# A fused attention and feed-forward kernel: GpSimd's join of the global probabilities moves to the next slot, and a tile's output split moves ahead of the maxima

## The chip, the cores and the metric

The kernel runs on one core of a Trainium2 chip. Its time is the device time of one execution in microseconds (us), lower is better. A core has a matrix engine (PE, with its weight loads shown apart as PEld), a vector engine (DVE), a scalar engine (ACT), GpSimd (POOL) and a sync engine (SP) that here issues nearly all transfers. Each engine works through its own instructions in order; between engines, semaphores make one wait for another.

## The reference

Attention over 8 batches and 8 heads of size 64, with 512 local tokens and 32 global tokens each, followed by a feed-forward layer on all 4352 rows. Global queries see every key; local queries see the 32 global keys and the local keys at most 32 positions away.

```python
s_g = scale * np.matmul(q_g, k_all.transpose(0, 1, 3, 2))
out_g = np.matmul(sm(s_g), v_all)                  # 32 global queries, 544 keys
s_ll = np.where(mask, scale * q_l @ k_l.T, -1e9)   # mask: |i - j| <= 32
s_l = np.concatenate([scale * q_l @ k_g.T, s_ll], axis=-1)
out_l = np.matmul(sm(s_l), np.concatenate([v_g, v_l], axis=2))
x = concat([out_g, out_l]).transpose(0, 2, 1, 3).reshape(4352, 512)
h = np.maximum(x @ w_in, 0.0)                      # 512 -> 2048
out = (h * h) @ w_out                              # 2048 -> 512
```

## The kernel before

**Tiles and slots.** A tile is 256 local queries of one head, so there are 16 groups (batch and half of the sequence) of 8 heads, 128 tiles in all. The main loop (line 605) runs one slot for each t from 0 to 145. Slot t begins tile t's attention, ends that of tile t-1, and runs step m = t-9 of the feed-forward layer: 17 blocks of 256 rows with 8 steps each (16 blocks of local rows, and a last one of the 256 global rows). Block k uses the outputs of group k. The last of its tiles, 8k+7, gets its output split (`x_evac`, line 278) in slot 8k+9, the very slot of the block's step 0; these are the slots with t % 8 == 1.

**Precision.** From tile 16 on, products are made of float32 split into two float32r parts. ACT writes the high part by a copy that rounds, DVE the rest by a subtraction. So each tile has pairs of such instructions: `qk` (queries and keys), `v` (values), `ph`/`pl`/`ml` (probabilities), `gh`/`gl` (hidden values), `x_h`/`x_l` (outputs).

**One slot, engine by engine** (from slot 17 on every engine keeps the order in which the program is written, `InOrder`, line 43):

- PE: the scores of tile t (`s<-qk`, line 155), the first product of the step (`h<-x_h`, `h<-x_l`, 24 matmuls in two halves, line 463), a score of the global queries (`gs`), the second product of the step before (`o<-ws`, 12 matmuls, line 497), then `av` of tile t-1 (`xa<-ph`, `xa<-ml`, `xa<-pl`, line 250). Some slots have one `g_av` (`gxo`, 13 matmuls) between the two halves of the second product.
- DVE: the two masked maxima of tile t (`softmax1`, writing `prob` from the scores), `x_l` of tile t-2, the rest of `v`, the normalisation (`softmax3`), then the jobs of place 3, then `parts_rest` of tile t-1 (`ph` on 32 partitions, `ml`, `pl`), `split_qk_rest` of tile t+1 (two subtractions named `qk`), in odd slots `g_evac` (`sg<-gs`), and `gl`.
- ACT: `x_h`, the high part of `v`, the two exponentials, the high part `ph`, jobs of place 3, the high part `qk` of tile t+1, the two activations of the hidden values (`pt<-h`, `pt<-pt`) and `gh`.
- POOL: `join` of tile t-1, one copy that puts the turned planes together again (`joined<-turned`), then `turn` of tile t, three copies that take the normalised probabilities apart into two 16-bit planes (`planes<-prob`).
- SP: the transposing DMA of tile t (`turned<-planes`, issued in `turn`), the load of tile t+2, and loads and stores of other jobs.

The transposition of a tile's probabilities is thus: `prob` normalised by DVE, three POOL copies, a DMA, one POOL copy in the next slot, ACT's `ph`, DVE's parts, and `av` on PE near the end of that slot.

**Global queries.** Four heads of a batch make one unit of 32 x 4 = 128 rows and 544 keys, 16 units in all, two for each batch. Its scores are gathered in `sg` over the slots before. Its other work is put into slots by a table by hand (line 680): each entry has a slot, a place in the slot, and a function. The slot d is t for the first unit of a batch and t+2 for the second, so that the units of batch after batch have their slot d+2 at t % 16 = 13 and 3. Places 4 and 3 come behind `load_head` (line 641), place 2 behind `g_evac`, places 0 and 1 inside and behind the second product. The entries that matter here:

```python
(d + 2, 3, g_norm),         # DVE: sum, reciprocal; then g_turn
(d + 3, 3, g_split_v, 0),   # ACT gvh, DVE gvl and gvh
(d + 3, 2, g_parts),        # ACT pth, DVE ptl and pth
(d + 3, 2, g_load_v, 1),
(d + 4, 0, g_av, 0),        # PE gxo
```

`g_turn` (line 374), called by `g_norm`, does for a unit what `turn` and `join` do for a tile, and does it in one go: a POOL copy of `sg` into planes (`gp<-sg`), a transposing DMA (`gq<-gp`) that SP issues behind the tile's own and behind a load, and a POOL copy back into `sg` (`sg<-gq`). POOL's next instruction is `join` of the same slot's tile, in slot d+3. I call slot d+2 the norm slot, d+3 the join slot and d+4 the parts slot.

Of the kernel before, what the change touches and what calls it, by code (L numbers as in the profile page):

```python
# [10 lines left out]
U16 = mybir.dt.uint16  # L11
# [9 lines left out]
NT = NGR * H  # L21
# [8 lines left out]
NPLAIN = 16  # L30
# [8 lines left out]
def f(ap):  # L39
    return ap.bitcast(F32)  # L40
# [19 lines left out]
def attention_moe(  # L60
# [22 lines left out]
    def plain(t):  # L83
        return t < NPLAIN
# [3 lines left out]
    def w_take(n):  # L88
        w_bufs["free"] -= n

    def load_head(t):
        if plain(t):
            w_take(1)
            raw = wp.tile([P, 1024], F32, tag="w", name=f"raw{t}")[:, :PK]
        else:
            raw = p2.tile([P, PS], F32, tag="raw", name=f"raw{t}")
        if t == 0:
            nc.sync.dma_start(raw[:, : QC + KC], pk[t, :, : QC + KC])
        else:
            sp.dma_start(raw, pk[t, :, : raw.shape[1]])  # L100
        heads[t] = dict(raw=raw)
# [16 lines left out]
    sg = cp.tile([P, 2, 640], F32, name="sg")  # L118
# [30 lines left out]
    def split_v(t):  # L149
        raw = heads[t]["raw"]  # L150
        v = heads[t]["v"] = p2.tile([P, 2, 192], F32R, tag="v", name=f"v{t}")
        ac.copy(v[:, 0, :], raw[:, QK:])
        ve.tensor_sub(v[:, 1, :], raw[:, QK:], f(v[:, 0, :]))

    def scores(t):
        hd = heads[t]
        pool, tag = (ps_h, "h") if t < 8 and t % 2 else (ps_a, "s")
        s = pool.tile([P, 2, WIN], F32, tag=tag, name=f"s{t}")
        for u in range(2):
            qs, ks = slice(KC + u * P, KC + u * P + P), slice(128 * u, 128 * u + WIN)  # L160
            if plain(t):
                pe.matmul(s[:, u, :], hd["raw"][:, qs], hd["raw"][:, ks], start=True, stop=True)
            else:
                pe.matmul(s[:, u, :], hd["hi"][:, qs], hd["hi"][:, ks], start=True, stop=False)
                pe.matmul(s[:, u, :], hd["lo"][:, u * P : u * P + P], hd["hi"][:, ks], start=False, stop=True)
        hd["s"] = s
# [46 lines left out]
    def transposes(t):  # L213
        pr = heads[t]["pr"]
        for i, (o, n) in enumerate(((0, 128), (320, 128), (128, 96), (224, 96))):
            pe.transpose(pt[:n, 128 * i : 128 * i + 128], pr[:, o : o + n], ident)

    def pt_copy(t):
        pts = p2.tile([P, 512], F32, tag="gh", name=f"pts{t}")
        ac.copy(pts, pt)  # L220
        heads[t]["pts"] = pts
# [9 lines left out]
    def join(t):  # L231
        words = joined.bitcast(U16).rearrange("p (n h) -> p h n", h=2)
        po.tensor_copy(words, turned.rearrange("p (h c) n -> p h (c n)", h=2))
# [4 lines left out]
    def parts(t):  # L238

        ph = heads[t]["ph"] = p1.tile([P, 512], F32R, tag="ph", name=f"ph{t}")  # L240
        ac.copy(ph, joined)
# [36 lines left out]
    def x_evac(t):  # L278
        g, h = divmod(t, 8)
        xa = heads[t]["xa"]  # L280
        r = slice((h % 2) * 64, (h % 2) * 64 + 64)
        if g == 0:
            ac.copy(xg[r, h // 2, :], xa)
        else:
            ac.copy(x_h[r, g % 2, h // 2, :], xa)
            ve.tensor_sub(x_l[r, g % 2, h // 2, :], xa, f(x_h[r, g % 2, h // 2, :]))
        heads[t] = None

    state = {}
# [84 lines left out]
    def g_turn(t, s):  # L374

        a = p1.tile([P, 1280], U16, tag="pth", name=f"gp{t}")
        z = p1.tile([P, 10, P], U16, tag="ptl", name=f"gq{t}")
        words = s.bitcast(U16).rearrange("p (n h) -> p h n", h=2)
        po.tensor_copy(a.rearrange("p (h n) -> p h n", h=2), words)
        sp.dma_start_transpose(out=z, in_=a)  # L380
        po.tensor_copy(words, z.rearrange("p (h c) n -> p h (c n)", h=2))

    def g_parts(t):
# [194 lines left out]
    def w_need(m):  # L578

        if m < 8:  # L580
            while w_next["bits"] < 8 * m + 8:
                n = w_next["bits"]
                w_pass()
                assert w_next["bits"] > n
        elif m < 16:
            while not set(range(4 * (m - 8), 4 * (m - 8) + 4)) <= whi.keys():
                n = w_next["split"]
                w_chunk()
                assert w_next["split"] > n, (m, w_next, w_bufs, sorted(w_used)[-1:])
# [15 lines left out]
    for t in range(NSTEP + LAG + 1):  # L605
        m = t - LAG
        ve.on, ac.on, pe.on, po.on, sp.on = [t >= x for x in FREE]
        prev, run = 1 <= t <= NT, 0 <= m < NSTEP
        live, early = t < NT, t < NPLAIN
        if t < NPLAIN - 8:  # L610
            load_head(t + 8)
        if run:
            w_need(m)
        old = prev and plain(t - 1)
        new = prev and not old
        if old:
            transposes(t - 1)
        if new:
            join(t - 1)
        if live and not early:  # L620
            scores(t)
        if old:
            pt_copy(t - 1)
        if live:
            softmax1(t)
        if NPLAIN <= t - 2 < NT:
            x_evac(t - 2)
        if run:
            gemm1(m, 0)
        if live and not early:  # L630
            split_v(t)
        if live:
            softmax2(t)
        if new:
            parts(t - 1)
        if live and not early:
            softmax3(t)
            turn(t)
        if NPLAIN <= t + 2 < NT:
            load_head(t + 2)  # L640
        for place in (4, 3):
            for job, *args in jobs.pop((t, place), ()):
                job(*args)
        if 0 < m <= NSTEP and m % 8 == 1 and m > 8:
            evac(m // 8 - 1)
        w_tick(t, 0)
        if live and early:
            g_scores(t)
        if run:
            gemm1(m, 1)  # L650
        if old:
            av(t - 1)
        if live and not early:
            g_scores(t)
        if early and t + 1 < NPLAIN:
            scores(t + 1)
        if t + 1 < NT and not early:
            split_qk(t + 1)
        if run:
            act1(m)  # L660
        if old:
            x_evac(t - 1)
            w_take(-1)
        if early:
            softmax3(t)
        w_tick(t, 1)
        if t + 1 == NPLAIN:
            split_qk(t + 1)
        if new:
            parts_rest(t - 1)  # L670
        if t + 1 < NT:
            split_qk_rest(t + 1)
        if live:
            if t % 2 == 1:
                g_evac(t)
            if t % 4 == 3 and t + 1 < NT:
                g_load(t + 1)
        if live and t % 4 == 3 and (t // 8) % 2 == 1:
            d = t if t % 8 == 3 else t + 2
            for at, *job in (  # L680
                (d, 2, g_load_v, 0),
                (d + 1, 3, g_soft),
                (d + 1, 1, g_exp),
                (d + 2, 3, g_norm),
                (d + 3, 3, g_split_v, 0),
                (d + 3, 2, g_parts),
                (d + 3, 2, g_load_v, 1),
                (d + 4, 0, g_av, 0),
                (max(d + 5, 17), 3, g_x, 0),
                (d + 5, 2, g_split_v, 1),  # L690
                (max(d + 6, 17), 0, g_av, 1),
                (max(d + 7, 18), 3, g_x, 1),
            ):
                place, job, *args = job
                jobs.setdefault((at, place), []).append((job, t, *args))
        for job, *args in jobs.pop((t, 2), ()):
            job(*args)
        if m == NSTEP:
            for i in range(2):
                gemm2(m - 1, 0, (i,))  # L700
                gemm2(m - 1, 1, (i,))
                evac(NBLK - 1, (i,))
        elif m > 0:
            gemm2(m - 1, 0)
        for job, *args in jobs.pop((t, 0), ()):
            job(*args)
        if 0 < m < NSTEP:
            gemm2(m - 1, 1)
        if new:
            av(t - 1)  # L710
        if run:
            act2(m)
        w_tick(t, 2)
        for job, *args in jobs.pop((t, 1), ()):
            job(*args)
        if 0 < m <= 8:
            w_done(m - 1)
        w_tick(t, 3)
        if 8 * NGR - 2 <= m < 8 * NGR:
            cols = (slice(0, 224), slice(224, HALF))[m % 2]  # L720
            ac.copy(x_h[:, 0, :, cols], xg[:, :, cols])
            ve.tensor_sub(x_l[:, 0, :, cols], xg[:, :, cols], f(x_h[:, 0, :, cols]))
# [75 lines left out]
```

## Time and profile before

| what | value |
|---|---|
| median of 3 runs | 1126.45 us (1126.15 to 1127.83) |
| the profiled execution | 1123.84 us |
| its span, first to last instruction | 1122.1 us |
| mean granted PE clock over the span | 0.963 |
| busy: PE, PEld | 1052.1, 927.1 us |
| busy: DVE, ACT, POOL | 829.5, 720.4, 373.6 us |

Times in the trace are counted from the start of the span. A line of the timeline has start, duration, engine, source line (nearly all have line 53, that of the recording helper, so one goes by the names of tiles), operation, what is written from what, shapes and a count; in brackets stands how long the engine stood idle just before, and what ended that wait. A line of the windows view has a stretch of time, its length, the busy time of each engine in it with the number of its instructions, the granted PE clock (1.00 is full), the DMA engines' share and their GB/s. A line of the waits view has who waited for whom, the total, the count and the longest.

### The profile page before, as it was taken

What the parts mean: (1) busy time and instruction counts of PE and PEld (TensorE: products, weight loads), DVE (VectorE), ACT (ScalarE), POOL (GpSimd) and SP (SyncE); (2) the same over time, 40 slices, a digit from 0 to 9 for tenths busy, and PEclk for the clock granted to TensorE, in tenths of its full rate; (3) what the DMA queues carried; (4) which work ended last, traced back from release to release, by engine and by line L of the source; (5) the groups of instructions that cost most, each with busy time, mean ns of one, the idle gap of its engine ahead of it and who ended that gap; (6) DMA issues with size and microseconds to landing.
All of it is one profiled execution on the core that took longest, in us unless ns stands there. A gap on an engine that the chain in (4) does not pass through costs nothing.

```text
span 1122.1 us, 20557 instructions
## 1 busy us (share of the span) xinstructions
PE 1052.1 (94%) x7040; PEld 927.1 (83%) x7040; DVE 829.5 (74%) x2477; ACT 720.4 (64%) x1743; POOL 373.6 (33%) x496
## 2 busy tenths in 40 slices
PE   8999879998998989999998989989899899989998
PEld 6776669887997979878887879978798779979987
DVE  5688877787877878877887878878688878873310
ACT  6888667666776756766676666757576666654332
POOL 1001234433344343444344343443343433441000
PEclk9999989999999989989899999989899999989999
DMA  9782434455344544534445344445345354432000
GB/s 373 272 286 56 105 96 105 101 122 118 94 112 97 129 98 112 128 98 108 108 107 112 98 117 111 119 98 124 89 110 120 98 121 107 116 81 52 14 19 19
DMA packets 193576, 127.69 MB, mean 114 GB/s; under 512 B 143552, under 2 KB 168640, under 8 KB 193472
## 3 DMA queue, kind: packets, MB, share of 16 engines
q1 hardware_dynamic: 193328, 126.32, 43.8%
q8 instruction: 55, 0.90, 0.3%
q14 instruction: 49, 0.40, 0.1%
q10 hardware_dynamic: 144, 0.07, 0.0%
HBM read 82.84 MB, written 8.91 MB: 82 GB/s over the span
## 4 chain that ended last, share of the span: by engine, by line
PE 62%; DVE 14%; DMA 8%; ACT 6%; issue 6%; POOL 2%; SPq 0%; DVEq 0%; POOLq 0%; ACTq 0%
PE h L53 24%; PE o L53 23%; DMA gq<-gp 6%; PE s L53 6%; PE xa L53 5%; DVE prob L53 3%; PE gxo L53 2%; POOL joined L53 2%; DVE qk L53 2%; DVE ml L53 2%; PE gs L53 1%; DVE x_l L53 1%; DMA raw<-in_pk_dram 1%; DVE pl L53 1%; DVE st L53 1%
## 5 line engine op out<-in xcount | busy, mean ns | idle before, releaser
L53 PE MATMUL h<-x_h,ws 128*128 128x256 f32 x2048 | 409.0, 292 | 0.0
L53 PEld LDWEIGHTS h<-x_h,ws 128*128 128x128 f32 x2048 | 344.8, 201 | 0.7
L53 PE MATMUL o<-ws,gh 128*128 128x512 f32 x1024 | 322.6, 396 | 1.5 <-ACT ot L53 1.5
L53 PE MATMUL h<-x_l,ws 128*128 128x256 f32 x1024 | 299.9, 293 | 3.2 <-DVE x_l L53 3.2
L53 POOL COPY joined<-turned 128x1024 uint16<-128x1024 uint16 x112 | 158.8, 1418 | 321.0 <-DMA turned<-planes 123.8
L53 POOL COPY planes<-prob 128x448 uint16<-128x448 uint16 x336 | 163.3, 523 | 189.6 <-DVE prob L53 189.6
L53 PEld LDWEIGHTS h<-x_l,ws 128*128 128x128 f32 x1024 | 206.1, 201 | 6.7 <-DVE x_l L53 6.0
L53 PEld LDWEIGHTS o<-ws,gh 128*128 128x128 f32 x1024 | 182.6, 188 | 34.0 <-ACT ot L53 2.0
L53 PE MATMUL o<-ws,gl 128*128 128x512 f32 x512 | 201.8, 394 | 0.0
L53 ACT ACTIVATE prob<-prob,st 128x224 f32<-128x224 f32 x224 | 106.3, 476 | 88.2 <-DVE st L53 88.0
L53 DVE TENSOR_TENSOR gl<-pt,gh 128x512 fp32r<-128x512 f32 x128 | 88.1, 688 | 83.1 <-ACT gh L53 80.9
L53 PE MATMUL xa<-ph,v 128*64 128x128 f32 (+1 forms) x672 | 77.4, 247 | 46.6 <-DVE ph L53 24.2
L53 ACT CAST ph<-joined 128x512 fp32r<-128x512 f32 x112 | 68.3, 610 | 81.7 <-POOL joined L53 81.4
L53 ACT ACTIVATE pt<-h 128x512 f32<-128x512 f32 x128 | 74.5, 582 | 70.0 <-PE h L53 69.1
L53 DVE TENSOR_TENSOR qk<-raw,qk 64x352 fp32r<-64x352 f32 x224 | 113.0, 504 | 7.8 <-ACT qk L53 0.8
L53 DVE CUSTOM_DVE_ANT_0 prob<-s,con 128x224 f32<-128x224 f32 x224 | 78.2, 386 | 54.8 <-PE s L53 54.4
L53 PEld LDWEIGHTS xa<-ph,v 128*64 128x64 f32 x672 | 57.9, 137 | 69.4 <-ACT ph L53 28.4
L53 PEld LDWEIGHTS o<-ws,gl 128*128 128x128 f32 x512 | 96.0, 188 | 22.9
L53 ACT CAST x_h<-xa 64x256 fp32r<-64x256 f32 x120 | 43.7, 364 | 99.8 <-PE xa L53 99.2
L53 PE MATMUL s<-qk 128*128 128x224 f32 x448 | 89.5, 314 | 6.2 <-DVE qk L53 3.7
L53 ACT CAST qk<-raw 128x608 fp32r<-128x608 f32 x112 | 78.2, 698 | 9.6 <-DMA raw<-in_pk_dram 9.5
L53 PEld LDWEIGHTS s<-qk 128*128 128x128 f32 x448 | 66.1, 202 | 16.3 <-DVE qk L53 15.3
(86 smaller groups left out, 1585.4 us busy)
## 6 DMA issues: line engine op xcount, KB each, us to landing
raw<-in_pk_dram SPq DMA_DIRECT2D x112, 400.0 KB, 3.5
wr<-in_w_dram SPq DMA_DIRECT2D x32, 512.0 KB, 7.8
gv<-in_vg_dram SPq DMA_DIRECT2D x32, 320.0 KB, 3.7
out_dram<-ot SPq DMA_DIRECT2D x32, 256.0 KB, 2.5
raw<-in_pk_dram SPq DMA_DIRECT2D x15, 432.0 KB, 8.3
qr<-in_qg_dram SPq DMA_DIRECT2D x31, 64.0 KB, 3.2
turned<-planes SPq DMA_TRANSPOSE x112, 3.0
out_dram<-ot SPq DMA_DIRECT2D x8, 64.0 KB, 1.7
```

Of the source, the lines that this page charges most:

```text
L53: r = method(*args, **kwargs)
```

## The change

The last copy of `g_turn` becomes a function of its own, `g_join`, with an entry in the table for place 3 of the join slot, behind `g_split_v`; there it stands behind `join` of the tile before and behind the three copies of `turn` of the slot's own tile. `g_parts` goes from place 2 of the join slot to place 3 of the parts slot. And `x_evac` of tile t-2 (ACT's `x_h`, DVE's `x_l`) is written ahead of `softmax1` of tile t; on ACT that changes no order, since `softmax1` has nothing there, and on DVE `x_l` now stands ahead of the two maxima.

```diff
@@ def g_turn(t, s):
         po.tensor_copy(a.rearrange("p (h n) -> p h n", h=2), words)
         sp.dma_start_transpose(out=z, in_=a)
+        state["gq"] = z
+
+    def g_join(t):
+        words = sg[:, (t // 4) % 2, :].bitcast(U16).rearrange("p (n h) -> p h n", h=2)
+        z = state["gq"]
         po.tensor_copy(words, z.rearrange("p (h c) n -> p h (c n)", h=2))
...
         if old:
             pt_copy(t - 1)
+        if NPLAIN <= t - 2 < NT:
+            x_evac(t - 2)
         if live:
             softmax1(t)
-        if NPLAIN <= t - 2 < NT:
-            x_evac(t - 2)
         if run:
             gemm1(m, 0)
...
                 (d + 2, 3, g_norm),
                 (d + 3, 3, g_split_v, 0),
-                (d + 3, 2, g_parts),
                 (d + 3, 2, g_load_v, 1),
+                (d + 3, 3, g_join),
+                (d + 4, 3, g_parts),
                 (d + 4, 0, g_av, 0),
```

## The prediction

> **What bounds the kernel now.** I read the page first, then the waits, then the windows view by slots, and last the timeline of one unit.
>
> ```profile
> PE 1052.1 (94%) x7040; PEld 927.1 (83%) x7040; DVE 829.5 (74%) x2477; ACT 720.4 (64%) x1743; POOL 373.6 (33%) x496
> ...
> PE 62%; DVE 14%; DMA 8%; ACT 6%; issue 6%; POOL 2%; SPq 0%; DVEq 0%; POOLq 0%; ACTq 0%
> PE h L53 24%; PE o L53 23%; DMA gq<-gp 6%; PE s L53 6%; PE xa L53 5%; DVE prob L53 3%; PE gxo L53 2%; POOL joined L53 2%; DVE qk L53 2%; DVE ml L53 2%; PE gs L53 1%; DVE x_l L53 1%; DMA raw<-in_pk_dram 1%; DVE pl L53 1%; DVE st L53 1%
> ```
>
> PE looks full, but the chain that ended last leaves it for the transposition of the global probabilities (`gq<-gp`). The windows show what that costs: one plain slot, then a join slot and the sum of 13, then a parts slot and the sum of 12, last the first steady unit (slots 20 and 21). I cut slots where the scores' first matmul starts.
>
> ```profile
> 431.33:438.28 6.95, 6.95 (x53) 6.34 (x52) 5.67 (x20) 4.53 (x11) 2.56 (x4) 1.00 0.43 104
> ...
> 524.31:535.74 11.43, 8.25 (x53) 6.70 (x51) 6.23 (x21) 5.60 (x13) 3.98 (x5) 0.94 0.51 103
> sum 148.88, PE 107.53 PEld 86.60 DVE 80.94 ACT 71.75 POOL 51.79; mean PE 8.27 PEld 6.66 DVE 6.23 ACT 5.52 POOL 3.98
> ...
> 535.74:546.10 10.36, 10.36 (x63) 9.55 (x64) 8.66 (x21) 5.34 (x14) 3.71 (x5) 0.74 0.42 101
> sum 118.95, PE 118.47 PEld 108.90 DVE 106.15 ACT 65.90 POOL 43.78; mean PE 9.87 PEld 9.08 DVE 8.85 ACT 5.49 POOL 3.65
> ...
> sum 26.73, PE 18.19 PEld 15.66 DVE 16.45 ACT 12.68 POOL 7.18; mean PE 9.10 PEld 7.83 DVE 8.22 ACT 6.34 POOL 3.59
> ```
>
> A plain slot is 6.95 us and PE is busy in all of it. A join slot is 148.88/13 = 11.45 us with 8.27 busy: 4.50 too long. A parts slot is 118.95/12 = 9.91; 0.80 of its excess is the 13 `gxo` matmuls (a row below prices them), so 2.16 is loss, and there PE is "busy" because its clock is 0.74. A unit loses 6.66 us in these two slots. The last row: slots 20 and 21 lose 26.73 - 13.90 - 0.80 = 12.0.
>
> The timeline of the unit at 522 shows how (POOL's, PE's, ACT's and DVE's rows; the join slot begins at 524.31):
>
> ```profile
> 522.04 1.64 POOL L53 COPY gp<-sg 128x1280 uint16<-128x1280 uint16 x1
> 528.87 1.64 POOL L53 COPY sg<-gq 128x1280 uint16<-128x1280 uint16 x1 [5.18 <-DMA gq<-gp]
> 530.41 1.32 POOL L53 COPY joined<-turned 128x1024 uint16<-128x1024 uint16 x1
> 531.65 1.19 POOL L53 COPY planes<-prob 128x448 uint16<-128x448 uint16 x3
> 536.07 1.88 POOL L53 COPY joined<-turned 128x1024 uint16<-128x1024 uint16 x1 [3.22 <-DMA turned<-planes]
> ...
> 532.44 0.45 PE L53 MATMUL xa<-ph,v 128*64 128x128 f32 x4 [1.46 <-ACT ph L53]
> 534.54 0.69 PE L53 MATMUL xa<-ph,v 128*64 128x256 f32 x2 [1.65 <-DVE ph L53]
> ...
> 531.77 0.62 ACT L53 CAST ph<-joined 128x512 fp32r<-128x512 f32 x1 [4.46 <-POOL joined L53]
> 532.29 0.72 ACT L53 CAST gvh<-gv 128x640 fp32r<-128x640 f32 x1
> ...
> 522.60 1.92 DVE L53 TENSOR_TENSOR qk<-raw,qk 64x352 fp32r<-64x352 f32 x2
> 525.84 0.38 DVE L53 CUSTOM_DVE_ANT_0 prob<-s,con 128x224 f32<-128x224 f32 x1
> 527.75 0.58 DVE L53 TENSOR_SCALAR prob<-prob,st 128x224 f32<-128x224 f32 x2
> 533.05 0.69 DVE L53 TENSOR_TENSOR gvl<-gv,gvh 128x512 fp32r<-128x512 f32 x1 [4.72 <-ACT gvh L53]
> 536.06 0.68 DVE L53 TENSOR_TENSOR ptl<-sg,pth 128x512 fp32r<-128x512 f32 x1
> 536.76 1.28 DVE L53 TENSOR_TENSOR pth<-sg,pth 64x128 fp32r<-64x128 f32 x1
> ```
>
> POOL stands 5.18 us before a copy nobody needs yet; the tile's `joined` is queued behind it, ACT's `ph` behind that, DVE's and PE's work behind `ph`. Then both DVE splits of the unit are done while PE waits, and the half clock follows in the parts slot.
>
> **The change, part by part.**
>
> *`g_join` one slot later.* Removed from in front of `joined`: the wait and 1.6 us of copy. By the tile's own transposition `joined` would be ready early: at 536.07 it began 3.2 us after its `planes` ended, and in the norm slot `planes` ended at 522.1 (`gp` follows it), so it can start near 525.3 in place of 530.41, and `ph` right behind the exponentials. Added behind `planes` of the join slot: the same copy. `gq` lands, by POOL's row, at 528.87; the three `planes` follow the normalisation, which ended at 528.33, so `g_join` begins near 529.5 and ends near 531.1. The next `joined` needs its DMA, 3.2 us after `planes`, near 532.7. So POOL itself hides `g_join`; no DMA moves on SP's queue, as `g_join` issues none; but the load of `gv` for pair 1 still waits for DVE's `gvh`, and is wanted two slots later.
>
> *What is late next: DVE.* A plain slot's DVE rows:
>
> ```profile
> 432.13 0.39 DVE L53 CUSTOM_DVE_ANT_0 prob<-s,con 128x224 f32<-128x224 f32 x1 [1.13 <-PE s L53]
> 434.05 0.58 DVE L53 TENSOR_SCALAR prob<-prob,st 128x224 f32<-128x224 f32 x2
> 434.55 0.84 DVE L53 STREAM_TRANSPOSE xg<-gxs 32x32 f32<-32x32 f32 x4
> 436.67 0.98 DVE L53 TENSOR_TENSOR qk<-raw,qk 64x352 fp32r<-64x352 f32 x2
> 439.09 0.39 DVE L53 CUSTOM_DVE_ANT_0 prob<-s,con 128x224 f32<-128x224 f32 x1 [0.84 <-PE s L53]
> ```
>
> `qk` is done at 437.65 and the next scores start at 438.28: 0.63 of slack with 0.84 of transposes in the slot, so some 1.4 us may be added ahead of `qk` for nothing. The join slot adds `gvl` 0.69 and `gvh` 0.28 with gaps (1.0), and DVE enters it late: its maxima started at 525.84, 1.53 after the scores, not 0.80.
>
> To this comes a price that the old order hid. Beside `gp` (522.04 to 523.68) the pair `qk` took 1.92, in the plain slot 0.98; beside `joined` the 64x128 `pth` took 1.28. A DVE subtraction of two SBUF tiles that meets a POOL copy waits for its end. `sg<-gq` stood in DVE's idle 4.72 us; `g_join` will stand beside `gvl`, `gvh`, `ph`. Bounds: nothing, if it falls in the wait for ACT's `gvh`, to 1.64; I take 1.3, since it starts about when `gvl` ends. The Trainium skill's "SBUF — State Buffer" (the shared port pair) says the same as a rule, that a DVE instruction with two SBUF inputs and a GpSimd one that reads SBUF exclude each other and the loser waits for the whole instruction. By that rule the 1.64 would be the sum's term, 0.3 a unit more.
>
> So DVE reaches the end of `qk` in the join slot 1.0 + 1.3 + 0.8 (late entry) = 3.1 later than plain, against 1.4 of slack: 1.7 us of loss in place of 4.50.
>
> *`g_parts` in the parts slot.* ACT's `pth` 0.72 lies in ACT's slack (5.5 busy). DVE gets `ptl` 0.68 and `pth` 0.3 to 1.28 ahead of `ph`, `qk`; `gxo` gives PE 0.80 more. 1.0 + 0.3 (copies of `planes` beside them) - 0.8 - 1.4 is under zero, but DVE comes in late from the join slot. `gxo` stands behind the 24 `h` and half of the 12 `o`:
>
> ```profile
> 590.89 2.88 PE h L53 x24
> 593.91 2.80 PE o L53 x12
> ```
>
> With 0.5 for the scores it begins 4.9 us after them and needs DVE's `pth` only for its last matmul, near 5.6. The normalisation ends 3.3 after the scores (434.63); ACT's `pth`, 0.72 behind `ph`, and the two DVE splits bring me to 5.0 to 5.3, an estimate. I take 0.5 of loss in place of 2.16, bounds 0 and 2.2; most of the 2.16 was the half clock. In the slot after, DVE has 0.84 of transposes against the same slack: 0.
>
> So a unit loses about 2.2 where it lost 6.66: **4.45 gained**, 13 times (57.9; the parts slot missing among the 12 is taken like the others). Slots 20 and 21 carry weight splits (`ws`) on DVE as well; I take 4.5 lost of 12.0: **7.5 gained**. The unit of slot 13 lies in the phase that waits for weights, and the last, after the last tile, has no `joined` behind it: 0.
>
> *`x_l` ahead of the maxima.*
>
> ```profile
> PEld h L53 <- DVE x_l L53: 6.0, 14, 0.9
> PE h L53 <- DVE x_l L53: 3.2, 13, 0.7
> ...
> sum 51.50, PE 50.35 PEld 44.86 DVE 40.95 ACT 35.33 POOL 21.94; mean PE 7.19 PEld 6.41 DVE 5.85 ACT 5.05 POOL 3.13
> sum 50.06, PE 48.05 PEld 43.12 DVE 40.33 ACT 31.55 POOL 18.82; mean PE 8.01 PEld 7.19 DVE 6.72 ACT 5.26 POOL 3.14
> sum 54.29, PE 54.29 PEld 49.97 DVE 49.23 ACT 38.92 POOL 21.99; mean PE 7.76 PEld 7.14 DVE 7.03 ACT 5.56 POOL 3.14
> ```
>
> The sums are of the windows of slots t % 16 = 9 (7 of them, 7.36 each), 1 (6, 8.34) and 7 (7, 7.76). The last has 13 `gxo` and no loss, so `gxo` costs 0.80. Slots 9 and 1 are those where a block begins and PE waits for `x_l`: 0.41 and 0.58 too long. `x_l` will come some 0.7 earlier. I count 0.40 x 7 + 0.28 x 6 = **4.5 gained**; slot 1 gets half, as it starts with DVE late. Against it: the maxima wait for ACT's `x_h` and for `x_l`, 0.42 later where DVE is behind, 0.2 elsewhere (they wait 1.13 for the scores anyway); in a plain slot the 1.4 of slack covers it; in the join slot it is in the late entry.
>
> Sum: 57.9 + 7.5 + 4.5 = 69.9 less than the profiled execution's 1123.84 (span 1122.1 and 1.7 around it): 1053.9. The median of the runs is 2.6 above that execution, so I expect about **1055** between the two.
>
> **The rivals.**
>
> *PE's clock keeps falling.* The 1.7 us of join-slot loss still leaves PE idle in pieces. Speaking for it: pieces of 1.46 and 1.65 were enough for a parts slot at 0.74. A second mechanism of the same size goes with it: when DVE is late, the next `joined` slips between the two `qk` and holds the second for 1.3. Then a unit loses 4.7, and 13 x 1.96 = 25, 3 in slots 20 and 21 and 4 from `x_l` are gained: 1093. Against it, a slot with 0.98 of PE idle that kept its clock:
>
> ```profile
> 575.11:583.30 8.19, 7.21 (x53) 6.41 (x52) 6.28 (x16) 5.51 (x13) 3.13 (x4) 1.00 0.44 124
> ```
>
> The Trainium skill's "TensorE: Matmul & The Clock Gate" (what's actually happening) has the clock fall after an idle window of some 3.4 us; by that rule this rival would not occur, yet here two pieces of under 1.7 us sufficed. Chance 0.2.
>
> *All the loss goes.* If DVE's work is hidden wholly, a unit loses 0.5: 13 x 6.16 + 9.5 + 6 = 96, giving about 1030. For it: slots with 0.84 of transposes and a later split of `gv` still take 6.95. Chance 0.16.
>
> *The change doesn't free `joined`.* If `gq` landed after the next `joined` is due, POOL would wait as now, one slot later; it needs a landing 7 us or more after SP's issue.
>
> ```profile
> DMA to landing us min/median/max: 3.1/4.6/6.1
> ```
>
> The longest is 6.1, so chance 0.03, and the time 1115 to 1124.
>
> *Slower.*
>
> ```profile
> L53 ACT CAST x_h<-xa 64x256 fp32r<-64x256 f32 x120 | 43.7, 364 | 99.8 <-PE xa L53 99.2
> ...
> L53 DVE TENSOR_TENSOR x_l<-xa,x_h 64x256 fp32r<-64x256 f32 x120 | 49.7, 414 | 4.8 <-ACT x_h L53 3.0
> ```
>
> The maxima now stand behind `x_h` (0.36) and `x_l` (0.42). If nothing hid the two, each of 112 slots would lose 0.78, 87 us, against 65 from the units and slots 20 and 21: 1146. It turns against the kernel from 0.6 a slot. The 1.13 and 0.84 for which the maxima wait for scores, while `x_h` is ready, speak against it. Chance 0.03.
>
> **How the numbers follow.** Forecast 1055, chance 0.58; 1030: 0.16; 1093: 0.2; no release 0.03; slower 0.03. The forecast's own range, by its bounds of 1.0 to 3.3 a unit, is 1038 to 1070. The range for 8 in 10 takes in most of both neighbours: 1033 to 1093. About 0.2% (2.3 us) is what a measurement can tell from no change. Faster 0.95, same 0.02, slower 0.03.
>
> **What would show it.** Right: POOL's `sg<-gq` without a long wait, standing behind `planes`; `joined` of the norm slot's tile starting about 1 us after the scores; join slots of about 8.6 us and parts slots of 8.2; `gvl` or `gvh` or `ph` stretched beside `sg<-gq`; the wait of `h` for `x_l` nearly gone; plain slots still 6.95. Wrong: join slots over 10 us, a granted clock below 0.9 in parts slots, or plain slots above 7.0, which would be `x_l` on the path.

## The result, and the profile after

The changed kernel takes 1080.92 us (median of 4 runs, 1076.66 to 1085.06) against 1126.55 for the kernel before on the same chip: a ratio of 0.9593 [0.9555, 0.9631]. The profiled execution is the 1076.66. Forecast were 1055 and a range of 1033 to 1093. So the sign and the range held, and the size did not: the span fell by 1122.1 - 1074.9 = 47.2 us where 69.9 were forecast.

From the page of the changed kernel, the busy times and the shares of the chain that ended last:

```profile
PE 1031.6 (96%) x7040; PEld 908.9 (85%) x7040; DVE 853.1 (79%) x2477; ACT 718.1 (67%) x1743; POOL 382.1 (36%) x496
...
PE 41%; DVE 30%; ACT 13%; issue 7%; DMA 5%; POOL 4%; POOLq 0%; SPq 0%; DVEq 0%; ACTq 0%
PE o L53 17%; PE h L53 16%; DVE qk L53 5%; ACT prob L53 5%; DVE prob L53 4%; DVE ml L53 4%; DMA turned<-planes 4%; PE xa L53 3%; PE s L53 3%; DVE gl L53 3%; POOL joined L53 2%; DVE st L53 2%; ACT ph L53 2%; DVE x_l L53 2%; POOL planes L53 2%
```

The wait for `gq<-gp` (6% of the chain before) is no longer among the chain's items, as intended. But PE holds 41% of the chain where it held 62%, and the rest is not one engine: it runs through the tile's probabilities, `prob`, `planes`, `turned`, `joined`, `ph`, `ml`. That loop had a far smaller part of the chain before.

The view of cores gives span and mean granted clock, first of the kernel before, then of the changed one:

```profile
core 0: 1122.1 us, clock 0.963
```

```profile
core 0: 1074.9 us, clock 0.990
```

If PE was busy all the time that its clock was low, it lost (1 - 0.963) x 1122.1 = 41.5 us before and (1 - 0.990) x 1074.9 = 10.7 after. PE's busy time for the same 7040 matmuls fell by 1052.1 - 1031.6 = 20.5. So between 20 and 31 of the 47 us came back as clock, and the rest as fewer waits.

The first unit's join slot, by POOL's and DVE's rows of the timeline (the slot runs from 581.82 to 590.34), and its row in the windows view:

```profile
582.54 1.36 POOL L53 COPY joined<-turned 128x1024 uint16<-128x1024 uint16 x1 [1.81 <-DMA turned<-planes]
585.83 1.71 POOL L53 COPY planes<-prob 128x448 uint16<-128x448 uint16 x3 [1.93 <-DVE prob L53]
587.49 1.81 POOL L53 COPY sg<-gq 128x1280 uint16<-128x1280 uint16 x1
...
587.31 0.51 DVE L53 TENSOR_TENSOR ph<-joined,ph 32x256 fp32r<-32x256 f32 x1
587.85 1.55 DVE L53 TENSOR_TENSOR ml<-joined,ph 64x128 fp32r<-64x128 f32 x1
```

```profile
581.82:590.34 8.52, 7.85 (x50) 6.52 (x51) 7.63 (x21) 5.05 (x13) 4.83 (x5) 1.00 0.67 125
...
sum 59.65, PE 54.53 PEld 45.64 DVE 53.67 ACT 36.32 POOL 34.07; mean PE 7.79 PEld 6.52 DVE 7.67 ACT 5.19 POOL 4.87
...
sum 48.89, PE 48.36 PEld 43.56 DVE 42.38 ACT 35.08 POOL 18.43; mean PE 8.06 PEld 7.26 DVE 7.06 ACT 5.85 POOL 3.07
```

`joined` starts 0.72 us after the scores, `sg<-gq` stands behind `planes` with no wait at all, and one of DVE's subtractions beside it, `ml`, takes 1.55 in place of 0.28. It is so in six of the first units' seven join slots; in the seventh it is the first `qk` that meets the copy (1.78 in place of 0.52). The two sums are the first units' seven join slots, 59.65/7 = 8.52, and six parts slots, 48.89/6 = 8.15.

A table of mean slot lengths shows where the time came from and where it went. Each is the mean distance between the first matmuls of the scores of slots t and t + 1, over t = 29 to 126 (6 or 7 slots in a row of the table); classes not shown differ by 0.02 at most. E1 is the changed kernel with `x_l` put back behind the maxima.

| t % 16 | before | after | E1 |
|---|---|---|---|
| 14, join, first unit | 11.26 | 8.52 | 8.22 |
| 15, parts, first unit | 9.83 | 8.15 | 8.15 |
| 4, join, second unit | 11.67 | 9.74 | 9.03 |
| 5, parts, second unit | 9.99 | 9.23 | 8.78 |
| 9 and 1, a block begins | 7.36, 8.34 | 6.95, 7.88 | 7.36, 8.27 |
| 10 and 2, the slots behind them | 7.16, 6.95 | 8.24, 7.53 | 7.03, 6.95 |
| 13 and 3, norm | 7.44, 7.06 | 7.44, 7.25 | 7.54, 7.06 |
| slots 29 to 126, sum of all | 796.2 | 756.6 | 741.2 |
| slots 16 to 28, sum | 110.8 | 105.6 | 103.3 |

Slots 9 and 1 gained what they should, and slots 10 and 2 gave it back twice over: 1.08 + 0.58 against 0.41 + 0.46.

### The profile page after: what moved, and what is told of

It reads as the page before. It is cut to its first block, busy times and chain, and to the rows that moved or that the text cites. A ratio compares the mean times of both kernels' runs of the same rounds, so it can differ in the third digit from the quotient of the medians.

```text
span 1074.9 us, 20570 instructions
## 1 busy us (share of the span) xinstructions
PE 1031.6 (96%) x7040; PEld 908.9 (85%) x7040; DVE 853.1 (79%) x2477; ACT 718.1 (67%) x1743; POOL 382.1 (36%) x496
## 4 chain that ended last, share of the span: by engine, by line
PE 41%; DVE 30%; ACT 13%; issue 7%; DMA 5%; POOL 4%; POOLq 0%; SPq 0%; DVEq 0%; ACTq 0%
PE o L53 17%; PE h L53 16%; DVE qk L53 5%; ACT prob L53 5%; DVE prob L53 4%; DVE ml L53 4%; DMA turned<-planes 4%; PE xa L53 3%; PE s L53 3%; DVE gl L53 3%; POOL joined L53 2%; DVE st L53 2%; ACT ph L53 2%; DVE x_l L53 2%; POOL planes L53 2%
## 5 line engine op out<-in xcount | busy, mean ns | idle before, releaser
L53 PE MATMUL h<-x_h,ws 128*128 128x256 f32 x2048 | 395.6, 286 | 0.0
L53 PEld LDWEIGHTS h<-x_h,ws 128*128 128x128 f32 x2048 | 332.9, 194 | 0.7
L53 PE MATMUL h<-x_l,ws 128*128 128x256 f32 x1024 | 293.0, 286 | 0.0
L53 POOL COPY joined<-turned 128x1024 uint16<-128x1024 uint16 x112 | 155.9, 1392 | 323.9 <-DMA turned<-planes 192.9
L53 POOL COPY planes<-prob 128x448 uint16<-128x448 uint16 x336 | 170.0, 543 | 211.6 <-DVE prob L53 211.6
L53 PEld LDWEIGHTS h<-x_l,ws 128*128 128x128 f32 x1024 | 199.3, 195 | 1.3 <-DVE x_l L53 0.2
L53 PE MATMUL s<-qk 128*128 128x224 f32 x448 | 85.9, 304 | 9.8 <-DVE qk L53 6.8
L53 PEld LDWEIGHTS s<-qk 128*128 128x128 f32 x448 | 63.3, 194 | 20.4 <-DVE qk L53 19.7
L53 ACT ACTIVATE pt<-pt 128x512 f32<-128x512 f32 x128 | 74.5, 582 | 4.1
L53 ACT CAST gh<-pt 128x512 fp32r<-128x512 f32 x128 | 74.6, 583 | 2.4
```

The costliest lines, as they stand in the source:

```text
L53: r = method(*args, **kwargs)
```

## The experiments

Two theories stood at the start. By the first, `x_l` ahead of the maxima costs time all through the loop. By the second, the missing 22 us lie in the units (the lock of DVE by the join, or the clock), and `x_l` is harmless.

### E1 and E2: each half of the change without the other

E1 is the changed kernel with the old place of `x_evac`. E2 is the kernel before with only `x_evac` moved.

```diff
 # E1, against the changed kernel
-        if NPLAIN <= t - 2 < NT:
-            x_evac(t - 2)
         if live:
             softmax1(t)
+        if NPLAIN <= t - 2 < NT:
+            x_evac(t - 2)
```

> The changed kernel with the output split back behind the maxima, all else kept. Theory A (read from the trace after): the early split saves 0.4 us in the slots where a block begins (t % 8 = 1) and gives back more in the slots after them, since maxima, normalisation and so the next joined come later and ACT's copy of the block's output stands behind ph, which waits for joined. Without it slots 9 and 1 are 0.4 longer (7.36 and about 8.3), slots 10, 2 and 3 return to 6.95 to 7.1, and maxima in the join slots come 0.4 earlier: 1066 to 1077 us. Theory B (my forecast): the early split is worth 4.5 us, so this kernel takes about 1085.

> The kernel before with only the output split moved ahead of the maxima. Theory A: gains of 0.4 in slots 9 and 1 are given back in slots 10 and 2: no gain, 1124 to 1134 us. Theory B (my forecast): 4.5 us gained, 1122.

E1 took 1060.35 us, 0.944 [0.9406, 0.9474] of the kernel before: 20 us less than the changed kernel. E2 took 1135.14, 1.0088 [1.0073, 1.0103]: alone, the move makes the old kernel 0.9% slower. Both lie outside theory A's ranges (1066 to 1077 and 1124 to 1134), on the side of a higher price. So `x_l` is not harmless: the move costs about 10 us in the old kernel, and 17 (by the ratios to the kernel before) to 20 (by the medians) in the changed one. Nor is the cost spread over all slots: by the table most plain slots keep their 6.95. In E2, too, slots 10 and 2 grow, to 8.08 and 7.53.

What it does shows in a slot 10 (t = 90) of the changed kernel, beginning at 674.57; DVE's, POOL's, ACT's and PE's rows:

```profile
675.17 0.42 DVE L53 TENSOR_TENSOR x_l<-xa,x_h 64x256 fp32r<-64x256 f32 x1 [0.51 <-ACT x_h L53]
675.51 0.37 DVE L53 CUSTOM_DVE_ANT_0 prob<-s,con 128x224 f32<-128x224 f32 x1
...
676.05 1.65 POOL L53 COPY joined<-turned 128x1024 uint16<-128x1024 uint16 x1 [3.21 <-DMA turned<-planes]
...
677.74 0.62 ACT L53 CAST ph<-joined 128x512 fp32r<-128x512 f32 x1 [0.77 <-POOL joined L53]
678.27 1.06 ACT L53 COPY ot<-o 128x512 f32<-128x512 f32 x2
...
678.90 0.73 PE L53 MATMUL o<-ws,gh 128*128 128x512 f32 x2 [0.66 <-ACT ot L53]
```

And the same slot of the kernel before, beginning at 704.93:

```profile
705.74 0.39 DVE L53 CUSTOM_DVE_ANT_0 prob<-s,con 128x224 f32<-128x224 f32 x1 [1.19 <-PE s L53]
...
705.75 1.37 POOL L53 COPY joined<-turned 128x1024 uint16<-128x1024 uint16 x1 [3.21 <-ACT v L53]
...
707.15 0.62 ACT L53 CAST ph<-joined 128x512 fp32r<-128x512 f32 x1
707.68 1.07 ACT L53 COPY ot<-o 128x512 f32<-128x512 f32 x2
```

The maxima start 0.94 us after the scores in place of 0.81. But `joined` starts at 1.48 in place of 0.82 and now waits for its DMA, `ph` waits for `joined`, `ot`, the copy of the block's output, stands behind `ph` on ACT, and PE's next `o` needs `ot`'s buffer. Where that lateness arises is read from the same rows of all six slots, as means of the time since the slot's first matmul of the scores. In slots 9 the normalisation ends 3.76 after the scores, before 3.29; and the slot itself is 0.41 shorter. The tile's copies and DMA take as long as before, so seen from slot 10 its probabilities land 0.47 + 0.41 = 0.88 later, and `joined` indeed starts at 1.98 there against 1.03 (0.91 in E1). Waits of the changed kernel (who waits for whom, total, count, longest):

```profile
DVE st L53 <- ACT prob L53: 41.4, 82, 0.5
...
ACT ph L53 <- POOL joined L53: 26.9, 35, 2.3
...
DVE x_l L53 <- ACT x_h L53: 23.9, 42, 0.9
...
PE o L53 <- ACT ot L53: 9.3, 9, 2.1
...
DVE prob L53 <- PE s L53: 1.3, 1, 1.3
...
PEld h L53 <- DVE x_l L53: 0.2, 1, 0.2
```

And three of the same rows of the kernel before:

```profile
DVE prob L53 <- PE s L53: 54.4, 64, 1.4
...
DVE st L53 <- ACT prob L53: 8.3, 40, 0.5
...
PE o L53 <- ACT ot L53: 1.5, 2, 1.0
```

`x_l` itself is now early: of the 6.0 us that PE's weight loads waited for it 0.2 are left. But DVE has paid for it. `x_l` used to fill the time in which DVE waits for the exponentials; now that wait is idle, 41.4 us in all where it was 8.3 (8.0 in E1), and `x_l` waits 23.9 for `x_h` where it waited 3.0. In return the maxima hardly wait for the scores any more, 1.3 where it was 54.4. The three waits come to 65.7 before, 60.2 in E1 and 66.6 in the changed kernel: DVE's idle time was moved far more than added. The move is a loss where the maxima had no wait for scores to lend, in slots that DVE enters late.

### E4: the block's output copied ahead of ACT's `ph`

If the cost in slots 10 and 2 is only `ot` behind `ph`, writing `evac` ahead of the parts of tile t-1 should give it back.

```diff
 # E4, against the changed kernel
+        if 0 < m <= NSTEP and m % 8 == 1 and m > 8:
+            evac(m // 8 - 1)
...
-        if 0 < m <= NSTEP and m % 8 == 1 and m > 8:
-            evac(m // 8 - 1)
```

> The changed kernel with ACT's copy of a finished block's output (ot) written ahead of the high part ph in its slot. Theory A: PE's wait for ot in slots 10 and 2 comes from ph, which waits for joined; with ot ahead of it both slots return to about 6.95, which is 8 to 10 us: about 1072. Rival: ot is late because the second product of the block before ends late, or ph then becomes late for av: no gain, 1078 to 1085.

It took 1076.92 us, 0.957 [0.9555, 0.9584], about the changed kernel's. Slots 10 and 2 were mended, 8.24 to 6.98 and 7.53 to 7.00; the view of windows, the six slots 10 of E4:

```profile
sum 41.86, PE 41.86 PEld 38.10 DVE 32.77 ACT 31.90 POOL 19.85; mean PE 6.98 PEld 6.35 DVE 5.46 ACT 5.32 POOL 3.31
```

But slots 12, 13 and 3 grew from 6.95, 7.44 and 7.25 to 7.28, 7.83 and 7.66, and the second unit's join and parts slots by 0.15 and 0.34. `joined` of slot 11 now starts 2.34 after the scores (0.93 in the changed kernel) and the maxima of slot 12 at 1.72 (0.98). So `ot` was where the lateness came to the surface, not its cause: without that wait the late chain runs on until another step meets it.

### E10 and E11: the early split only where a block begins, and everywhere else

```diff
 # E10, against E1 (in E11: t % 8 != 1)
+        early_x = t % 8 == 1
+        if early_x and NPLAIN <= t - 2 < NT:
+            x_evac(t - 2)
         if live:
             softmax1(t)
-        if NPLAIN <= t - 2 < NT:
+        if not early_x and NPLAIN <= t - 2 < NT:
             x_evac(t - 2)
```

> e1_no_x_move with the early output split only in slots with t % 8 = 1, where a block begins and PE waits for x_l. Theory A1: the loss of the early split lies in these slots themselves: being 0.4 shorter they bring the end of the block's old product, ot and the late joined closer together, so slots 10 and 2 lose 0.9 and 0.4 and join slots lose nothing: 1061 to 1066 us. Theory A2: the loss comes from later maxima in all slots; then this keeps the gain of 0.4 in slots 9 and 1 and loses little: 1054 to 1058.

> The complement: the early output split in all slots but those with t % 8 = 1. Theory A1: slots 10 and 2 stay near 6.95, slots 9 and 1 as in e1_no_x_move; only join slots and those around them lose 0.3 to 0.7: 1066 to 1072 us. Theory A2: slots 10 and 2 lose nearly as much as in the changed kernel: 1073 to 1080.

E10 took 1062.49 us, 0.9439 [0.9419, 0.9459]; E11 took 1079.18, 0.9588 [0.9561, 0.9615]. In E10 the slots 9 and 1 are 6.94 and 7.75, a gain of 0.42 and 0.52 on E1, and the slots 10 and 2 behind them 7.88 and 7.21, 0.85 and 0.26 longer: nothing is left of it even where `x_l` is wanted at once, as theory A1 has it. The windows of E10, slots 9, then slots 10:

```profile
sum 41.64, PE 41.64 PEld 38.15 DVE 34.62 ACT 29.91 POOL 18.82; mean PE 6.94 PEld 6.36 DVE 5.77 ACT 4.99 POOL 3.14
...
sum 47.26, PE 43.27 PEld 38.44 DVE 37.53 ACT 33.05 POOL 19.86; mean PE 7.21 PEld 6.41 DVE 6.25 ACT 5.51 POOL 3.31
```

E11 carries nearly the whole loss, in slots where nobody waited for `x_l`: against E1, slots 14 grow by 0.30, 12 by 0.30, 3 by 0.36, 4 by 0.70, 10 by 0.53. Its time lies in A2's range, E10's in A1's, so neither theory holds for both runs. In slots 14 it is DVE's own queue and not the longer chain: `joined` starts no later than in E1 (0.76 and 0.87 after the scores), the maxima 0.34 later (1.65 and 1.31).

### E3 and E5: what the join itself still costs

E3 is the changed kernel without the join: the global probabilities stay unturned, so the outputs of the global queries are not those of the reference. E5 is E1 with the copy done by ACT.

```diff
 # E3, against the changed kernel
-                (d + 3, 3, g_join),
 # E5, against E1, in g_join
-        po.tensor_copy(words, z.rearrange("p (h c) n -> p h (c n)", h=2))
+        ac.copy(words, z.rearrange("p (h c) n -> p h (c n)", h=2))
```

> The changed kernel without the copy sg<-gq: the global probabilities stay unturned, all that follows runs on them. If the copy beside DVE's subtractions is what is left of the loss in the join slots (ml 1.5 us in place of 0.28, qk waiting behind it), join slots fall by 1.2 us to about 7.3 (first unit of a batch) and 8.6 (second), 14 times: about 1062 us. If DVE is late there because of its own added work, the time stays within 4 us of 1081.

> e1_no_x_move with the copy sg<-gq done by ACT in place of POOL, at the same place of the program; nothing is left out. If it was the meeting of POOL's copy with DVE's subtractions that cost the join slots 1.2 us, they fall from 8.2 and 9.0 to about 7.3 and 8.0 as in e3_join_left_out, and ACT's own 1.3 us lies in its slack: 1042 to 1050 us. If the cost was only that the work has to be done somewhere, ACT is late for qk and the time stays within 4 us of 1060.

E3 took 1056.01 us, 0.9384 [0.937, 0.9398]; E5 took 1054.7, 0.937 [0.9349, 0.9391]. The first units' join slots fall from 8.52 to 7.35 in E3, and against E1's 8.22 to 7.50 in E5. So having the copy on POOL costs 1.17 in the changed kernel, against no copy at all, and 0.72 in E1, against ACT's copy. The windows of E3's seven join slots:

```profile
sum 51.47, PE 50.84 PEld 45.32 DVE 45.37 ACT 34.44 POOL 21.49; mean PE 7.26 PEld 6.47 DVE 6.48 ACT 4.92 POOL 3.07
```

Rows of an E5 join slot, ACT's copy and DVE's subtractions beside and behind it, and the windows of its seven join slots:

```profile
575.39 1.66 ACT L53 COPY sg<-gq 128x1280 uint16<-128x1280 uint16 x1 [0.18 <-DMA gq<-gp]
...
576.46 0.51 DVE L53 TENSOR_TENSOR ph<-joined,ph 32x256 fp32r<-32x256 f32 x1
577.00 0.28 DVE L53 TENSOR_TENSOR ml<-joined,ph 64x128 fp32r<-64x128 f32 x1
```

```profile
sum 52.52, PE 51.01 PEld 45.35 DVE 46.67 ACT 40.34 POOL 21.56; mean PE 7.29 PEld 6.48 DVE 6.67 ACT 5.76 POOL 3.08
```

The copy is as long on ACT (1.66) as on POOL (1.64 in the kernel before). But `ph` runs through under it in the 0.51 that it also took in the changed kernel's slot, and `ml`, where the changed kernel's subtraction stood for 1.55, takes 0.28. The copy is still made, and the stretch is gone: it came from POOL's being the one that copies. E5 pays elsewhere, and so comes out above the 1042 to 1050 that it was to reach: slots 16 to 28 take 109.6 in place of 103.3, where `gq` lands late and ACT waits in order for it:

```profile
140.93 1.61 ACT L53 COPY sg<-gq 128x1280 uint16<-128x1280 uint16 x1 [3.63 <-DMA gq<-gp]
```

### E6: the parts back in the join slot

```diff
 # E6, against E1
-                (d + 4, 3, g_parts),
+                (d + 3, 2, g_parts),
```

> e1_no_x_move with g_parts back at place 2 of the join slot, so that only the join moves. Theory A: the parts then stand behind qk in the join slot, make gl and the next maxima late by 1 us or more and ACT's pth waits for the join with gh behind it; the parts slot has 0.8 us of slack from gxo that is then unused: join slots about 8.5, parts slots 8.5 or more, 1064 to 1080 us. Theory B: DVE's work is the same in sum over the two slots, so nothing changes: 1056 to 1064.

It took 1077.75 us, 0.9567 [0.955, 0.9584], 14 (by the ratios) to 17 us more than E1, so this step of the change has a worth of its own. The join slot of the first unit hardly sees it (8.22 to 8.19, where 8.5 was expected). It is the slots behind that pay, 15 from 8.15 to 8.54 and 1 from 8.27 to 9.28, and the second unit's join slot, 9.03 to 9.56. PE's wait for `x_l`, in E6 and then in E1:

```profile
PE h L53 <- DVE x_l L53: 7.8, 14, 1.2
```

```profile
PE h L53 <- DVE x_l L53: 2.7, 13, 0.3
```

The two splits now run in the first 2.3 us of the parts slot, ahead of the maxima. There `pth` meets `joined` and takes 1.29 in place of 0.32 (11 times of 12), as the 64x128 `pth` did in the kernel before. The maxima of slots 15 start 2.95 us after the scores, 1.20 in E1, and two slots further on `x_l` starts at 2.66, 1.64 in E1. So a good part of what this step is worth is that `pth` no longer meets a POOL copy.

### E7: the second unit's join slot

The changed kernel's second units stayed worse than the first: 9.74 and 9.23 against 8.52 and 8.15. DVE's and POOL's rows at the start of one such join slot (it begins at 627.93), and its later rows:

```profile
628.67 1.35 POOL L53 COPY joined<-turned 128x1024 uint16<-128x1024 uint16 x1 [1.83 <-DMA turned<-planes]
...
628.85 1.27 DVE L53 TENSOR_TENSOR qgz<-qr,qgz 128x128 fp32r<-128x128 f32 x1
630.04 0.68 DVE L53 TENSOR_TENSOR gl<-pt,gh 128x512 fp32r<-128x512 f32 x1
630.64 0.41 DVE L53 TENSOR_TENSOR x_l<-xa,x_h 64x256 fp32r<-64x256 f32 x1
630.97 0.37 DVE L53 CUSTOM_DVE_ANT_0 prob<-s,con 128x224 f32<-128x224 f32 x1
...
635.35 1.53 DVE L53 TENSOR_TENSOR ml<-joined,ph 64x128 fp32r<-64x128 f32 x1
```

`qgz`, a part of the next unit's queries (`g_load`), is written near the end of the norm slot, runs over into the join slot and there meets the freed `joined`. The maxima then start 630.97 - 627.93 = 3.04 after the scores. The view of this tile alone (shortest, median and longest in ns) shows that 1.27 is not its normal length; the kernel before has 294 as its longest:

```profile
L53 DVE TENSOR_TENSOR qgz<-qr,qgz x28: 275/294/1360, 68.0 to 935.5; 128x128 fp32r<-128x128 f32 x28
```

E7 is E1 with `g_load` written ahead of `g_evac`, so that `qgz` comes before `joined` starts.

```diff
 # E7, against E1
-            if t % 2 == 1:
-                g_evac(t)
...
+            if t % 2 == 1:
+                g_evac(t)
```

> e1_no_x_move with the split of the global queries (qgz) written ahead of the sums into sg in slots with t % 4 = 3. Theory: in the second unit of a batch the norm slot (t % 16 = 3) has qgz, which in some slots meets joined and takes 1.26 in place of 0.29, so that the maxima of the join slot come 1 us late. Ahead of the sums it is over before joined starts: slot 4 falls from 9.03 to about 8.2 and slot 5 to 8.15, 6 to 8 us in sum: about 1053. Rival: the second unit is slower for its other reasons (one DVE sum more in the norm slot): no change, 1058 to 1063.

It took 1055.7 us, 0.9378 [0.9364, 0.9392]. The second unit's slots fell from 9.03 to 8.57 and from 8.78 to 8.15, and its parts slots kept their clock. The six second units of E1 say the same: where `qgz` was long (three times) the join slot took 9.55, in the others 8.40 to 8.60. In the changed kernel it was long five times. A slot of 9.9 takes the join's copy as well: in E3 `qgz` took 1.26 to 1.41 in all six, and the join slots are 8.67, still 1.32 above the first unit's. `qgz` in one of E7's norm slots:

```profile
614.96 0.28 DVE L53 TENSOR_TENSOR qgz<-qr,qgz 128x128 fp32r<-128x128 f32 x1
```

What the clock does is read from pairs, a second unit's join slot with the parts slot behind it. Two of them from the windows of the changed kernel, first the join slots, then the parts slots:

```profile
378.46:388.35 9.89, 8.11 (x50) 6.59 (x50) 8.94 (x21) 5.12 (x13) 4.82 (x5) 0.98 0.60 115
...
627.93:637.82 9.89, 8.06 (x50) 6.59 (x51) 8.94 (x21) 5.16 (x13) 4.81 (x5) 1.00 0.59 115
...
388.35:399.16 10.81, 10.81 (x64) 10.02 (x64) 7.64 (x21) 5.74 (x14) 4.41 (x5) 0.70 0.46 126
...
637.82:645.97 8.15, 8.06 (x63) 7.26 (x64) 7.13 (x21) 5.61 (x14) 3.07 (x4) 1.00 0.45 118
```

Two join slots of 9.89 with 1.78 and 1.83 us of idle PE were followed by a clock of 0.70 and of 1.00. Of the six pairs, the five with 1.7 to 1.9 idle led four times to 0.70 to 0.84, the one with 1.07 kept its clock, and in E7, with 0.76 to 1.09, none of six lost it. Other runs blur this: with 1.5 of idle the clock fell after two of three such join slots in E1 and after four of six in E6, in E11 after only one of five with 1.8 but also after one with 1.07.

What decides is not the idle time of the slot. In every kept trace all falls begin on one grid of 3.41 us, and each lasts one, two or more whole steps of it (the last is cut off by the end). In the changed kernel those of the slots above begin at 265.07, 387.95, 514.24 and 882.88, 36, 37 and 108 steps of 3.413 apart. The step ahead of the second fall, and the fall:

```profile
384.54:387.95 3.41, 1.89 (x13) 1.16 (x11) 3.30 (x6) 1.81 (x4) 2.78 (x3) 1.00 0.38 75
387.95:394.78 6.83, 6.65 (x31) 6.30 (x31) 5.75 (x18) 3.49 (x9) 3.06 (x4) 0.50 0.39 112
```

PE was idle for 1.52 of the 3.41. Over the steps at full clock in slots 28 to 126 of all 13 traces, a fall followed each of the 23 with 1.8 us of idle PE or more, none with less than 1.07, and 21 of the 51 between. So what counts, in the main, is how much idle time falls into one step.

### E8 and E9: what worked, together

E8 is E5's copy on ACT with E7's order. In E9 the first two units of all, put into the table at t = 11 and 15 (join slots 14 and 20), keep POOL's copy.

```diff
 # E9, against E8, in g_join
-        ac.copy(words, z.rearrange("p (h c) n -> p h (c n)", h=2))
+        (po.tensor_copy if t < 16 else ac.copy)(words, z.rearrange("p (h c) n -> p h (c n)", h=2))
```

> e1_no_x_move with both edits of e5_join_on_act and e7_qgz_first. If both theories hold the gains overlap only where a late start of the join slot is absorbed: 1038 to 1046 us. If not, the better of the two.

> e8_act_and_qgz with the join of the first two units (slots 14 and 20) left on POOL. In e5_join_on_act ACT waited 3.6 us for the DMA gq in slot 20, and slots 16 to 28 took 6.2 us more than in e1_no_x_move, while the later slots took 12.6 less. If that wait is the whole of it, 6 us come back: 1045 to 1048 us. If not, 1050 to 1053.

E8 took 1052.26 us, 0.9346 [0.9332, 0.936], which is no clear gain on E5 and above the 1038 to 1046 forecast: its slots 29 to 126 come to the same 728.6 us as E5's. Slot 4 fell from 8.18 to 7.69, and slots 10, 12, 13, 15 and 3 took that back. E9 took 1046.61 (1043.45 to 1047.61), 0.9292 [0.9271, 0.9313], and is the fastest of all: 34 us less than the changed kernel. Slots 16 to 28 take 102.9 in it, 110.4 in E8. The two join slots are 7.39 and 7.68, the parts slots 7.86 and 8.34. Its view of cores:

```profile
core 0: 1041.7 us, clock 0.998
```

## Why the prediction was right, and where it was wrong

- **`joined` is freed by the later join: right.** It starts 0.87 us after the scores in the first units' join slots (mean), before 5.92, and in the slots from 29 on the join waits once, for 0.41.
- **DVE is late next, with a lock of 1.3: right.** `ml` took 1.55 in place of 0.28, which is 1.27 (the instruction hit is not `gvl`, `gvh` or `ph`, which I had named; they took 0.83, 0.33 and 0.51, in E3 without the copy as well). The late entry, forecast 0.8 over a plain slot's 0.80, is there: the maxima start at 1.65. The first unit's slots came to 8.52 and 8.15, forecast 8.6 and 8.2; its gain is 11.26 + 9.83 - 8.52 - 8.15 = 4.42 a unit, forecast 4.45.
- **All units alike: partly wrong.** I read the windows of both kinds of unit as one sum. The second kind gained 11.67 + 9.99 - 9.74 - 9.23 = 2.69, through `qgz` in the norm slot and a clock that still fell. In E1 it gained 3.85. Slots 16 to 28 gained 110.8 - 103.3 = 7.5 in E1, as forecast for slots 20 and 21, and 5.2 in the changed kernel.
- **"`x_l` ahead of the maxima: 4.5 gained": wrong in sign, and the step that failed.** The gain itself is there: slots 9 and 1 fell by 0.41 and 0.46, and the wait for `x_l` all but went. The price was mis-stated: I put it at nothing, and the step came to a loss of 17 to 20 us. I set the later maxima against 1.4 us of slack, which is the slack of `qk` before the next scores. The same delay also reaches the exponentials, the normalisation, `planes`, the DMA and `joined`, and that chain goes around from slot to slot with less slack, least in slots 10 and 2; and where DVE was late already it had no wait to lend. Without this step the forecast would have been 1126.45 - 65.4 = 1061; E1 took 1060.35. That this is so close is partly luck: its first units gained 11.26 + 9.83 - 8.22 - 8.15 = 4.72, its second ones 3.85, and 4.45 was forecast for both.
- **A reading of the profile before.** "Both DVE splits of the unit are done while PE waits" is true of `gvl` and `gvh` alone. `ptl` and `pth` ran from 536.06 on, in a parts slot in which PE was busy for all of the 10.36.
- **The signs I had named for wrong.** "Plain slots above 7.0, which would be `x_l` on the path" missed it: most plain slots stayed at 6.95, and the loss lay in the slots where something else was already late. "A granted clock below 0.9 in parts slots" did show, in second units.
- **The rivals.** "PE's clock keeps falling" (1093) was half true, for second units alone. "Slower", with the maxima behind `x_h` and `x_l`, named the right mechanism and priced it as an even charge on every slot; its cost was 17 to 20 us, not 87, and came in a few. "All the loss goes" (1030) needs the lock gone: E9 comes to 1046.61.

What stays open: why the clock fell after some steps with 1.1 to 1.8 us of idle PE and not after others, and how much of the 17 to 20 us is DVE's later queue and how much the longer chain. The table places the 756.6 - 741.2 = 15.4 us of slots 29 to 126: 10.7 in slots 10 and 2, 7.0 in slots 4 and 5, 2.1 in slots 14, less 4.8 gained in slots 9 and 1, and 0.4 in the others. No run separates the two causes within these slots, but for slots 14.

## What to carry to other kernels

When an instruction is moved ahead of another, follow the delayed one through its whole chain into the next iteration, transfers included, and look for the least slack on it, not only for the nearest consumer. An instruction that fills an engine's wait costs nothing there; moved ahead, it delays all that stands behind it wherever the engine is already late. When a copy on one engine is freed to run earlier, look at what it now runs beside, and price slots of different kinds one by one.

## What the hardware showed that was not expected

A DVE subtraction of two SBUF tiles that met a POOL copy was shown longer, so its length is no measure of its work: `ml` took 0.28 or 1.55, `qgz` 0.29 or 1.27, `pth` 0.32 or 1.29. The POOL copy was shown longer in the first of these meetings (`sg<-gq` 1.81, 1.64 in the kernel before), and not in the second (`joined` 1.35, elsewhere 1.36). For this strided copy of 128x1280 16-bit words ACT was as quick as POOL.

The clock of PE fell after idle time in pieces, none over 1.12 us in the slots 4 of the changed kernel. In slots 28 to 126 of all traces it was halved (0.50) for whole steps of a fixed grid of 3.41 us, each time after a step with 1.07 us or more of idle PE. One piece of 2.12 in slot 74 of the changed kernel, which the grid cuts in two (1.79 in one step), left the clock at 1.00.
